# The last product by seven products of halves for the last 1280 tokens

## The chip, the core and the metric

One core of a Trainium2 chip runs the whole program. The metric is the device time of one execution in microseconds (us). Engines are named as the profile names them: PE multiplies matrices (PEld loads its stationary operand), DVE, ACT and POOL work on elements, SP issues the DMAs. All run their own instructions in the order in which the program gives them, and wait for each other by semaphores.

## The reference

Three blocks follow each other: an attention over 32 memory slots, a gated layer of width 1536, and a second layer of width 2048. The change is in the second layer's last product, `g @ w_out`: 2304 tokens of 2048 gated values times 2048 x 512 weights.

```python
def _moe2_ref(x, w_in, w_out) -> np.ndarray:
    h = x @ w_in
    g = h * (1.0 / (1.0 + np.exp(-1.702 * h)))
    return (g @ w_out).astype(np.float32)
```

The weights arrive as float64.

## The kernel before, in words

Every product is made of three passes over operands that are split into two parts: hi is the operand rounded to the type that PE takes, lo is the float32 rest, and the passes are hi·hi, lo·hi and hi·lo. `hi_lo` makes the parts: an ACT copy gives hi, and `combine` (DVE or POOL, whichever a planner finds sooner) subtracts it from the source. `PASSES` names the three.

The order of all instructions on all engines is made beforehand by a planner, `Order`: streams of work with priorities yield an engine and an estimated duration, and the stream that can start first is written out. Costs are those of the functions `dve`, `act` and `pool`. The engines then keep that order, whatever the real durations are.

The product with `w_in` already goes by seven products of halves for four (the function `step` with `PRODUCTS`, line 1062 of the profile: matmuls of 384 columns). `gate` applies the activation and stores the gated values to a DRAM tensor `g2d`, by SP's queue. The same queue loads the weights' float64 words into two buffers `raw`, and loads the gated values back.

The last product is `proj2` (line 1170): 18 tiles of 128 tokens, each 16 chunks of 128 of the 2048 values, three passes, 512 columns: 864 matmuls. `load_gated` loads 384 tokens by half of the 16 chunks (1.5 MB) into `acc`; `split_gated` makes hi and lo of 128 tokens and 8 chunks at a time (elements 128x1024, PE's stationary operand; SBUF names attn, wab_hl, vhl and whl_a, whichever old buffer lends the room). The weights' chunks are decoded from float64 words by `decode_piece`, one chunk of 128 x 512 at a time: an ACT Abs, a max (DVE or POOL, line 392), three DVE instructions on bits (lines 396, 400 and 405), then hi by ACT (line 282) and lo (line 276). Ten chunks go to the buffer y, three to g, two to whl_b, the last to eff_b.

The first six tiles are the front: PE takes them by quarters of the chunks, chunk 0 to 3 for all six tiles, then 4 to 7, and so on, since the weights' chunks are still being decoded. The other twelve follow tile by tile. `proj2_out` copies a finished bank out by ACT (line 268), and four DMAs store it.

Of the kernel before, what the change touches and what calls it, by code (L numbers as in the profile page):

```python
# [8 lines left out]
F32 = mybir.dt.float32  # L9
F32R = mybir.dt.float32r  # L10
U32 = mybir.dt.uint32
AF = mybir.ActivationFunctionType
# [139 lines left out]
def tile_mem_attention_moe_moe2(  # L152
# [38 lines left out]
    NG2 = F2 // (G2 * P)  # L191
    N2 = 384
    NP = NT // (2 * N2)
    KH = F2 // P // 2

    N1 = 512
    HT = NT // 2
# [11 lines left out]
        return Slots([pl.tile(shape, dt, name=f"{name}{i}") for i in range(n)])  # L209

    g2d = dram.tile([F2, NT], F32, name="g2d")

    banks = [psum.tile([P, 512], F32, name=f"bank{i}") for i in range(8)]
    bank_m, bank_a = Slots(banks[:3]), Slots(banks[3:])
# [163 lines left out]
    def decode_piece(t, i, name, part, n, m):  # L378

        plain = name[:2] == ("wab", 0)  # L380
        if plain:
            wt[name] = yield "slot", wab0_s
            t = max(t, wt[name][1])
        raw = loaded.pop(("raw", i))
        lw, hw = (raw[0][:, :, j].rearrange("p (n f) -> p n f", n=n) for j in range(2))
        mf = m[0].rearrange("p (n f) -> p n f", n=n)
        mu = mf.bitcast(U32)

        t, _ = yield ACT, t, act(512)
# [13 lines left out]
        t, _ = yield DVE, t, dve(512)  # L403
        dst = wt[name][0].rearrange("p (n f) -> p n f", n=n) if plain else mf
        nc.vector.scalar_tensor_tensor(
            out=dst.bitcast(U32), in0=lw, scalar=29, in1=mu, op0=ALU.logical_shift_right, op1=ALU.bitwise_or
        )
        raw_of(i).release(raw, t)
        if plain:
            dm_s.release(m, t)  # L410
            od.mark(t, *name, part)
        elif name[0] == "in":
            decoded[name, part] = m
            od.mark(t, "decoded", name, part)
            if part == 1:
                od.spawn(PW if name[1] else PW0, combine_weights(name[1]))
        elif name[0] == "o2":
            c = name[1]
            t = max(t, (yield "mark", "room", *name))
            t = yield from hi_lo(t, wo2[c][:, HI], wo2[c][:, LO], m[0], DM)  # L420
            dm_s.release(m, t)
            od.mark(t, "wo2", c)
        else:
            if part == 0:
                wt[name] = yield "slot", slots_of[name[0]]
                od.mark(wt[name][1], "place", name)
            t = max(t, (yield "mark", "place", name))
            yield from split_weights(t, name, part, wt[name][0], m, dst, n)
# [267 lines left out]
    def give(slots_, views):  # L696
        slots_.free += [[x, now()] for x in views]
# [199 lines left out]
        "P5": (S1, T1), "P6": (S2, T2), "P7": (S3, T3),  # L897
    }
    yc, win, wo2 = {}, {}, []
    win_s, hb_s, f_s, sb_s = Slots(), Slots(), Slots(), Slots()  # L900
# [5 lines left out]
    CN, FN, SN = 2 * DM, KH * N2, 2 * KH * P  # L906

    def parted(flat):

# [5 lines left out]

    def spare():
        return next(x for x in (whl_a, big["whl_b"]) if x is not wt["o1", NG1 - 1][0])

    def place(p, operands):
        for b in operands:  # L920
# [19 lines left out]
    def room_kept():  # L940

        n = KD * 2 * N2
        for r in range(2):
            yield "mark", "yc", 0, r
        give(hb_s, views(acc, N2, 6))
        give(dm_s, views(acc, DM, 1, 6 * N2))
        for r in range(2):
            yield "mark", "yc", 1, r
        give(hb_s, views(acc, N2, n // N2, n))
        for r in range(2):  # L950
            yield "mark", "yc", 2, r
        give(f_s, views(acc, FN, 1, 2 * n))

    def room_gated():

# [2 lines left out]
    def room_projected():  # L958

        nonlocal p2  # L960
        p2.release()
        p2 = tc.alloc_tile_pool(name="p3", bufs=1, reuse_waits="tile")
        rest = p2.tile([P, 6 * YN], F32R, name="rest")
        for i, x in enumerate(views(rest, YN, 6), 19):
            yc[2][i // 4][i // 2 % 2][i % 2] = x
        place(2, range(7))
# [4 lines left out]
            wo2.append(x.rearrange("p (i f) -> p i f", i=2))  # L971

    def room_split(*flat):
        give(sb_s, [x.rearrange("p (i c t) -> p i c t", i=2, c=KH) for x in flat])

    def room_last():

        used = wt["o1", NG1 - 1][0]
        room_chunks(*views(g1_m, CN, 3), *views(used, CN, 2), *views(big["eff_b"], CN, 1))
        room_split(*views(big["wab"], SN, 2), big["vhl"], spare())  # L980
# [138 lines left out]

    units = list(range(0, NT, N2))

    FRONT = 2
    parts = [(i, h) for h in range(2) for i in range(FRONT)]
    parts += [(i, h) for i in range(FRONT, len(units)) for h in range(2)]

    def load_gated():
        n = KH // G2
        for i, h in parts:  # L1130
            for g in range(h * n, (h + 1) * n):
                for j in range(2):
                    t = yield "mark", "g2", (g, i // 2), j, i % 2
            s = yield "slot", f_s
            f = s[0].rearrange("p (c t) -> p c t", c=KH)
            o = units[i]
            nc.sync.dma_start(
                out=f, in_=g2d[h * KH * P:(h + 1) * KH * P, o:o + N2].rearrange("(c p) t -> p c t", p=P)
            )
            od.load(max(t + 2500.0, s[1]), KH * P * N2 * 4, "f", i, h)  # L1140
            loaded["f", i, h] = s, f

    def split_gated():
        for i, h in parts:
            t = yield "mark", "f", i, h
            slot, f = loaded.pop(("f", i, h))
            for s in range(N2 // P):
                b = yield "slot", sb_s
                t2 = yield from hi_lo(max(t, b[1]), b[0][:, HI], b[0][:, LO], f[:, :, s * P:(s + 1) * P], KH * P)
                loaded["sb", i, h, s] = b  # L1150
                od.mark(t2, "sb", i, h, s)
            f_s.release(slot, t2)

    def proj2(tiles, cuts):

        ps = {}
        for o, e in cuts:
            h = o // KH
            for i, s in tiles:
                t = yield "mark", "sb", i, h, s  # L1160
                for c in range(o, e):
                    t = max(t, (yield "mark", "wo2", c))
                b = loaded["sb", i, h, s]
                if o == 0:
                    t, ps[i, s] = yield PE, t, 680 * (e - o), bank_m
                else:
                    t, _ = yield PE, t, 680 * (e - o)
                for c in range(o, e):
                    for n, (mv, sw) in enumerate(PASSES):
                        nc.tensor.matmul(  # L1170
                            ps[i, s][0], b[0][:, sw, c - h * KH, :], wo2[c][:, mv],
                            start=(c == n == 0), stop=(c == 2 * KH - 1 and n == 2),
                        )
                if e % KH == 0:
                    sb_s.release(b, t)
                if e == 2 * KH:
                    od.spawn(0, proj2_out(t, units[i] // P + s, ps[i, s]))

    def proj2_out(t, it, ps):
        m = yield "slot", dm_s  # L1180
# [26 lines left out]
    def main():  # L1207
# [79 lines left out]
        for q in order[1:]:  # L1287
            yield from quad(*q)
            if q == (NG2 - 1, 0):
                room_chunks(*views(big["y0"], CN, 10))  # L1290
            if q == (NG2 - 1, 1):
                room_split(*views(attn_m[0], SN, 2), *views(attn_m[1], SN, 2))
# [71 lines left out]
```

## Time and profile before

| what | us |
|---|---|
| median of 3 runs (lowest, highest) | 806.04 (805.52, 806.71) |
| profiled execution, its own time | 806.18 |
| its span, from the first to the last instruction | 804.40 |
| PE, busy | 782.6 |
| DVE, ACT, POOL, busy | 552.6, 386.6, 318.8 |
| last product on PE (line 1170) | 198.3 |

The span is what the trace shows; the profiled execution's own time is 1.78 us longer. Busy times add up per engine over stages of very different kinds, so the stage is what has to be read.

### The profile page before, as it was taken

How to read it: one execution, taken by the hardware profiler on the slowest of the kernel's cores; microseconds unless marked ns; L12 is line 12 of the kernel's file. 1: busy time of each engine (PE TensorE's matmuls, PEld its weight loads, DVE VectorE, ACT ScalarE, POOL GpSimd, SP SyncE). 2: the span in 40 equal slices, each digit the busy share in tenths (PEclk: the TensorE clock that was granted, in tenths of full speed). 3: DMA queues.
4: the chain of work that ended last, by engine and by line, in shares of the span. 5: the costliest groups of instructions: out<-in, count | busy, mean ns of one | idle time of the engine just before them, and what ended most of it. 6: DMA issues, size and time to landing. Idle time of an engine off the chain costs nothing. (4 is left out here: it accounts for less than half of the span.)

```text
span 804.4 us, 13239 instructions
## 1 busy us (share of the span) xinstructions
PE 782.6 (97%) x4928; PEld 703.0 (87%) x4928; DVE 552.6 (69%) x983; ACT 386.6 (48%) x839; POOL 318.8 (40%) x309
## 2 busy tenths in 40 slices
PE   8989999999999999999989999999999999999997
PEld 7777788899989899989978999999998878888886
DVE  4888978989988976964999877766795853212100
ACT  4567767554655545543765554554554542222200
POOL 1224235655634435432899474444376420000000
PEclk9999999999999999999999999999999999999999
DMA  8866401233230210220011326754559556323001
GB/s 292 305 205 195 147 1 53 80 105 109 76 105 28 80 52 27 67 66 1 1 45 49 136 79 214 249 170 161 170 167 342 168 198 211 115 81 118 23 17 39
DMA packets 59327, 95.48 MB, mean 119 GB/s; under 512 B 5248, under 2 KB 42112, under 8 KB 59264
## 3 DMA queue, kind: packets, MB, share of 16 engines
q1 hardware_dynamic: 58432, 93.84, 35.5%
q10 hardware_dynamic: 832, 0.82, 0.3%
q8 instruction: 38, 0.62, 0.3%
q14 instruction: 25, 0.20, 0.1%
HBM read 71.04 MB, written 23.59 MB: 118 GB/s over the span
## 5 line engine op out<-in xcount | busy, mean ns | idle before, releaser
L1104 DVE TENSOR_TENSOR acc<-bank,acc 128x384 f32<-128x384 f32 x168 | 86.9, 549 | 32.8 <-PE bank L1062 18.3
L1114 ACT ACTIVATE acc<-acc 128x384 f32<-128x384 f32 x96 | 48.1, 520 | 55.2 <-DVE acc L1104 54.9
L1170 PE MATMUL bank<-y,attn 128*128 128x512 f32 x300 | 70.8, 391 | 0.0
L1170 PEld LDWEIGHTS bank<-y,attn 128*128 128x128 f32 x300 | 56.3, 188 | 12.3
L276 POOL TENSOR_TENSOR y<-gr,y 128x288 fp32r<-128x288 f32 x43 | 37.7, 879 | 63.9 <-ACT y L282 63.7
L815 DVE TENSOR_TENSOR gr<-bank,gr 128x288 f32<-128x288 f32 x96 | 43.0, 449 | 25.6 <-PE bank L799 18.1
L832 PE MATMUL bank<-g,whl_b 128*128 128x288 f32 x384 | 55.6, 302 | 4.3 <-POOL g L276 2.0
L832 PEld LDWEIGHTS bank<-g,whl_b 128*128 128x128 f32 x384 | 53.3, 193 | 6.0 <-POOL g L276 2.8
L799 PE MATMUL bank<-attn,eff 128*128 128x288 f32 x384 | 55.2, 297 | 1.0 <-ACT eff L770 0.7
L276 DVE TENSOR_TENSOR attn<-acc,attn 128x1024 fp32r<-128x1024 f32 (+1 forms) x24 | 28.8, 1202 | 39.6 <-ACT attn L282 39.6
L799 PEld LDWEIGHTS bank<-attn,eff 128*128 128x128 f32 x384 | 52.2, 188 | 3.1 <-ACT eff L770 0.9
L812 ACT ACTIVATE gr<-bank 128x288 f32<-128x288 f32 x96 | 38.1, 399 | 32.3 <-PE bank L799 32.0
L276 POOL TENSOR_TENSOR g<-gr,g 128x288 fp32r<-128x288 f32 x37 | 35.6, 967 | 44.4 <-ACT g L282 44.1
L855 PE MATMUL bank<-y,whl_a 128*128 128x512 f32 (+1 forms) x240 | 51.5, 370 | 0.0
L855 PEld LDWEIGHTS bank<-y,whl_a 128*128 128x128 f32 x240 | 41.9, 188 | 8.0
L276 POOL TENSOR_TENSOR wab_hl<-dm,wab_hl 128x256 fp32r<-128x256 f32 (+1 forms) x31 | 29.3, 955 | 38.7 <-ACT wab_hl L282 36.4
L282 ACT ACTIVATE y<-gr 128x288 fp32r<-128x288 f32 x48 | 21.3, 444 | 43.5 <-DVE gr L815 43.3
L799 PE MATMUL bank<-attn,eff_b 128*128 128x288 f32 x288 | 40.8, 296 | 1.3 <-DVE acc L886 1.1
L875 DVE TENSOR_TENSOR acc<-bank,acc 128x512 f32<-128x512 f32 (+1 forms) x72 | 37.9, 548 | 5.1 <-PE bank L855 4.5
L799 PEld LDWEIGHTS bank<-attn,eff_b 128*128 128x128 f32 x288 | 39.0, 188 | 2.4 <-DVE acc L886 1.6
L390 ACT ACTIVATE dm<-raw 128x512 f32<-128x512 f32 x41 | 26.9, 667 | 23.5 <-DMA raw<-in_moe_w_b_dram 11.7
L392 POOL TENSOR_SCALAR dm<-dm 128x512 f32<-128x512 f32 x17 | 27.3, 1610 | 26.9 <-ACT dm L390 26.0
(287 smaller groups left out, 1941.1 us busy)
## 6 DMA issues: line engine op xcount, KB each, us to landing
g2d<-acc SPq DMA_DIRECT2D x96, 192.0 KB, 2.4
acc<-g2d SPq DMA_DIRECT2D x12, 1536.0 KB, 7.0
raw<-in_moe_w_out_dram SPq DMA_DIRECT2D x28, 512.0 KB, 4.0
raw<-in_moe_w_in_dram SPq DMA_DIRECT2D x16, 512.0 KB, 3.9
raw<-in_moe_w_a_dram SPq DMA_DIRECT2D x20, 256.0 KB, 2.8
raw<-in_moe_w_b_dram SPq DMA_DIRECT2D x20, 256.0 KB, 3.1
q<-in_q_dram SPq DMA_DIRECT2D x8, 576.0 KB, 6.4
out_dram<-dm SPq DMA_DIRECT2D x56, 64.0 KB, 1.7
```

The lines of the kernel that those rows point to most:

```text
L276: (nc.gpsimd if e == POOL else nc.vector).tensor_tensor(out=dst, in0=in0, in1=in1, op=op)
L390: nc.scalar.activation(out=mf, in_=hw.bitcast(F32), func=AF.Abs)
L392: (nc.vector if e == DVE else nc.gpsimd).tensor_scalar(out=mf, in0=mf, scalar1=2.0 ** -15, scalar2=None, op0=ALU.max)
L799: nc.tensor.matmul(ps[0][:, :U], e[c][:, sw, i * CW + j * P:i * CW + (j + 1) * P], attn(b, mv, c, u * U, U), start=(n == 0), stop=(n == 3 ...
L812: nc.scalar.activation(out=gr[0], in_=pa_[0][:, :U], func=AF.Copy)
L815: nc.vector.tensor_tensor(out=gr[0], in0=pb[0][:, :U], in1=gr[0], op=ALU.mult)
L832: nc.tensor.matmul(ps[0][:, :U], w[:, sw, j, mb * P:(mb + 1) * P], g1[0][:, j, mv, :], start=(n == 0), stop=(n == 3 * G1 - 1),)
L855: nc.tensor.matmul(ps[0][:, :e - o], w[:, sw, j, mb * P:(mb + 1) * P], g1_all[mv][:, j, o:e], start=(n == 0), stop=(n == 3 * G1 - 1),)
L875: nc.vector.tensor_tensor(out=dst, in0=ps[0][:, a - o:z - o], in1=dst, op=ALU.add)
L1104: nc.vector.tensor_tensor(out=s[0], in0=ps[0][:, :N2], in1=x[0], op=ALU.add)
L1114: nc.scalar.activation(out=c[0], in_=c[0], func=AF.Gelu_apprx_sigmoid)
L1170: nc.tensor.matmul(ps[i, s][0], b[0][:, sw, c - h * KH, :], wo2[c][:, mv], start=(c == n == 0), stop=(c == 2 * KH - 1 and n == 2),)
```

## The change

The first three units of 256 tokens (six tiles, the front) and a fourth unit are still multiplied tile by tile. The last five units (1280 tokens) are each taken as a 2 x 2 block product: two tiles of tokens, and even and odd chunks of each pair of chunks, against the halves of the 512 columns. `proj2_seven` makes seven products in place of eight, 24 matmuls of 256 columns each (two halves h of four chunk pairs, three passes), 840 matmuls for the five units. `sums_gated` makes the tokens' four sums (`MERGE`) and splits all seven operands. `sums_out` adds the products up: one ACT copy and seven DVE additions a unit.

The weights' sums T1 to T4 need float32 values of the weights. Each decoded chunk is now also written by SP's queue to a DRAM tensor `w2d` (256 KB), and `load_pair` reads two chunks at a time back (512 KB), makes four sums of 128x256 and splits each into hi and lo; both go into rooms that the older stage leaves (`blocks`). The chunk's buffer (dm) is kept until its write is done.

The operand buffers hold 4 chunks in place of 8 (`K4`): splits of 128x512, six slots of them. Loads of gated values are 256 tokens by 4 chunks (512 KB) in the front, and by 8 chunks (1 MB) after. From `room_last` on, the planner no longer puts DVE at a disadvantage against POOL (`W2`).

```diff
+W2 = 0.0
+PT = 28
...
-            t = yield from hi_lo(t, wo2[c][:, HI], wo2[c][:, LO], m[0], DM)
-            dm_s.release(m, t)
-            od.mark(t, "wo2", c)
+            nc.sync.dma_start(out=w2d[c * P:(c + 1) * P, :], in_=m[0])
+            od.mark(t + 2500.0, "w2d", c)
+            t2 = yield from hi_lo(t, wo2[c][:, HI], wo2[c][:, LO], m[0], DM)
+            dm_s.release(m, max(t + 2500.0, t2))
+            od.mark(t2, "wo2", c)
...
     def room_last():
 
+        od.handicap[DVE] = W2
...
-        give(f_s, views(acc, FN, 1, FN))
+        n = KD * 2 * N2
+        give(f_s, views(acc, FN, 1, n + 2 * FN))
+        give(fw_s, views(acc, 2 * FN, 1, n))
+        give(tb_s, views(acc, 2 * DM, 2))
+        for p in range(F2 // P // 2):
+            od.spawn(PT, load_pair(p))
+        yield "mark", "front"
+        give(fw_s, views(acc, 2 * FN, 2, n + 2 * FN))
...
+    MERGE = {
+        S1: (A22, A21, A22, ALU.add, (A22,)), S3: (A21, A11, A21, ALU.subtract, ()),
+        S2: (A11, A22, A11, ALU.subtract, (A11,)), S4: (A12, A12, A11, ALU.subtract, (A12,)),
+    }
+    HOME = {A11: A11, A12: A12, A22: A22, S1: A22, S3: A21, S2: A11, S4: A12}
+    LAST = ("P4", "P1", "P2", "P5", "P7", "P6", "P3")
...
+        for name in LAST:
+            a = PRODUCTS[name][0]
+            for h in (0, 2 * K4):
+                t, f = ts[h], parts[h][1]
+                if a in MERGE:
+                    dst, in0, in1, op, before = MERGE[a]
+                    for x in before:
+                        t = max(t, (yield "mark", "sw", i, h, x))
+                    ts[h] = t = yield from combine(t, f[dst], f[in0], f[in1], op, n)
+                yield from split_part(t, f[HOME[a]], "sw", i, h, a)
...
+    def load_pair(p):
+
+        t = max((yield "mark", "w2d", 2 * p), (yield "mark", "w2d", 2 * p + 1))
...
+        nc.sync.dma_start(
+            out=x.rearrange("p k j f -> p k (j f)"),
+            in_=w2d[2 * p * P:(2 * p + 2) * P, :].rearrange("(k p) f -> p k f", p=P),
+        )
...
+        for i, (dst, in0, in1) in enumerate(
+            ((b11, b12, b11), (b12, b22, b12), (b22, b22, b11), (b21, b21, b22))
+        ):
+            t = yield from combine(t, dst, in0, in1, ALU.subtract, n)
+            od.spawn(PT, split_t(t, wo2_t[p][i], dst, p, i))
...
+        for name in LAST:
+            a, b = PRODUCTS[name]
+            for h in (0, 2 * K4):
+                t = yield "mark", "sw", i, h, a
...
+                for c in range(K4):
+                    for n, (mv, sw) in enumerate(PASSES):
+                        nc.tensor.matmul(
+                            ps[name][0][:, :NB], x[0][:, sw, c, :], moving(b, h // 2 + c, mv),
+                            start=(h == c == n == 0), stop=(h > 0 and c == K4 - 1 and n == 2),
+                        )
...
-        tiles = [(i, s) for i in range(len(units)) for s in range(N2 // P)]
-        n = FRONT * N2 // P
-        yield from proj2(tiles[:n], [(o, o + KH // 2) for o in range(0, 2 * KH, KH // 2)])
-        for o in range(n, len(tiles), N2 // P):
-            yield from proj2(tiles[o:o + N2 // P], [(0, KH), (KH, 2 * KH)])
+        yield from proj2([(i, s) for i in range(NF) for s in range(2)])
+        for i in range(NF, NW):
+            yield from (proj2([(i, 0), (i, 1)]) if i < NS else proj2_seven(i))
```

How the change moves instructions, in three places. First PE, where the first unit by seven products begins. Before, the tiles behind the front go on with 512 columns:

```order
L1170 MATMUL bank_77<-y_1430,wab_hl 128x512 x24
L1170 MATMUL bank_76<-y_1430,wab_hl 128x512 x24
L1170 MATMUL bank_74<-y_1430,vhl 128x512 x24
L1170 MATMUL bank_77<-y_1430,whl_a 128x512 x6
L1170 MATMUL bank_77<-g_94,whl_a 128x512 x9
```

Now, behind the fourth unit's last chunks (y, g, whl_b and eff_b hold the weights' chunks; the other names hold their sums):

```order
L1287 MATMUL bank_77<-g_95,attn_92 128x512 x3
L1287 MATMUL bank_77<-whl_b,attn_92 128x512 x6
L1287 MATMUL bank_77<-eff_b,attn_92 128x512 x3
L1318 MATMUL bank_75<-wab_hl,attn_92 128x256 x6
L1318 MATMUL bank_75<-vhl,attn_92 128x256 x3
L1318 MATMUL bank_75<-whl_a,attn_92 128x256 x3
```

From there to the end every matmul has 256 columns.

Second DVE, at the decoding of the last chunk, the one that goes to eff_b. Before (dm and acc are the buffers of the chunk in decoding; vhl, wab_hl and attn are gated values being split):

```order
L405 SCALAR_TENSOR_TENSOR dm_84<-raw_78,dm_84 128x512
L276 TENSOR_TENSOR wab_hl<-acc,wab_hl 128x1024
L396 TENSOR_SCALAR acc<-acc 128x512
L400 SCALAR_TENSOR_TENSOR acc<-raw_79,acc 128x512
L405 SCALAR_TENSOR_TENSOR acc<-raw_79,acc 128x512
L276 TENSOR_TENSOR vhl<-acc,vhl 128x1024
```

Now (the rows of 128x256 are the weights' sums and their splits):

```order
L280 TENSOR_TENSOR whl_b<-acc,whl_b 128x512
L396 TENSOR_SCALAR dm_85<-dm_85 128x512
L400 TENSOR_SCALAR dm_85<-dm_85 128x512
L280 TENSOR_TENSOR acc<-acc 128x256
L404 SCALAR_TENSOR_TENSOR dm_85<-raw_79,dm_85 128x512
L280 TENSOR_TENSOR attn_92<-acc,attn_92 128x512
L280 TENSOR_TENSOR acc<-acc 128x256
L280 TENSOR_TENSOR eff_b<-acc,eff_b 128x256
L280 TENSOR_TENSOR acc<-acc 128x256
L280 TENSOR_TENSOR eff_b<-acc,eff_b 128x256
L409 SCALAR_TENSOR_TENSOR dm_85<-raw_79,dm_85 128x512
L280 TENSOR_TENSOR eff_b<-dm_85,eff_b 128x512
```

Sums of the weights stand between the steps of the last chunk's decoding, its max (line 396 there) is DVE's and no longer POOL's, and its lo is DVE's too.

Third SP's queue, at the raw loads of chunks 10 and 11. Before:

```order
L1116 DMA g2d<-acc 128x384 x4
L1137 DMA acc<-g2d 128x8x384 x2
L308 DMA raw_78<-in_moe_w_out_dram 128x1024
L308 DMA raw_79<-in_moe_w_out_dram 128x1024
L308 DMA raw_78<-in_moe_w_out_dram 128x1024
```

Now:

```order
L1141 DMA g2d<-acc 128x384 x3
L1156 DMA acc<-g2d 128x4x256
L1250 DMA acc<-w2d 128x2x512 x2
L312 DMA raw_80<-in_moe_w_out_dram 128x1024
L424 DMA w2d<-dm_84 128x512
L312 DMA raw_79<-in_moe_w_out_dram 128x1024
L424 DMA w2d<-dm_83 128x512
```

Two loads of 1.5 MB ahead of the raw loads have become one of 0.5 MB and two reads of `w2d`, and the writes of `w2d` stand between.

## Rows read from the trace of the kernel before

**Rows 1.** The page: busy time of each engine and its share of the span.

```profile
PE 782.6 (97%) x4928; PEld 703.0 (87%) x4928; DVE 552.6 (69%) x983; ACT 386.6 (48%) x839; POOL 318.8 (40%) x309
```

**Rows 2.** The chain that ended last, in order of time: start, length, what.

```profile
601.53 198.33 PE bank L1170 x864
```

**Rows 3.** Window: PE, PEld, DVE, ACT, POOL busy; clock, DMA share, GB/s.

```profile
600.00:650.00 50.00, 50.00 (x222) 41.24 (x221) 36.51 (x46) 23.09 (x32) 27.45 (x16) 1.00 0.75 262
```

**Rows 4.** Timeline around 652 us: start, length; the last weight chunk meets PE.

```profile
651.24 0.63 ACT L282 ACTIVATE eff_b<-acc 128x512 fp32r<-128x512 f32 x1 [3.38 <-DVE acc L405]
...
651.95 1.29 POOL L276 TENSOR_TENSOR eff_b<-acc,eff_b 128x512 fp32r<-128x512 f32 x1 [2.48 <-ACT eff_b L282]
...
652.94 1.08 PE L1170 MATMUL bank<-eff_b,vhl 128*128 128x512 f32 x3
```

**Rows 5.** Timeline of PE, the only three stretches of 256-column matmuls.

```profile
256.56 2.99 PE L855 MATMUL bank<-y,whl_a 128*128 128x256 f32 x24
...
312.15 2.92 PE L855 MATMUL bank<-y,whl_b 128*128 128x256 f32 x23
...
366.76 2.87 PE L855 MATMUL bank<-y,whl_a 128*128 128x256 f32 x23
```

**Rows 6.** Timeline of DVE, four instructions that follow each other.

```profile
633.62 0.43 DVE L396 TENSOR_SCALAR dm<-dm 128x512 uint32<-128x512 uint32 x1
634.08 0.69 DVE L400 SCALAR_TENSOR_TENSOR dm<-raw,dm 128x512 uint32<-128x512 uint32 x1
634.68 1.22 DVE L276 TENSOR_TENSOR attn<-acc,attn 128x1024 fp32r<-128x1024 f32 x1
635.82 1.10 DVE L405 SCALAR_TENSOR_TENSOR dm<-raw,dm 128x512 uint32<-128x512 uint32 x1
```

**Rows 7.** DVE's groups from 405 to 440 us, with POOL busy throughout: busy, mean ns.

```profile
L276 DVE TENSOR_TENSOR attn<-acc,attn 128x384 fp32r<-128x384 f32 x7 | 7.4, 1060 | 0.0
L1104 DVE TENSOR_TENSOR acc<-bank,acc 128x384 f32<-128x384 f32 x9 | 4.7, 544 | 0.0
```

**Rows 8.** DVE's groups from 601 to 655 us that hold most of its delay.

```profile
L400 DVE SCALAR_TENSOR_TENSOR dm<-raw,dm 128x512 uint32<-128x512 uint32 x6 | 5.2, 872 | 0.1
...
L405 DVE SCALAR_TENSOR_TENSOR dm<-raw,dm 128x512 uint32<-128x512 uint32 x6 | 5.0, 826 | 0.1
...
L396 DVE TENSOR_SCALAR acc<-acc 128x512 uint32<-128x512 uint32 x2 | 3.0, 1510 | 1.4 <-POOL acc L392 1.4
...
L405 DVE SCALAR_TENSOR_TENSOR acc<-raw,acc 128x512 uint32<-128x512 uint32 x3 | 2.7, 901 | 0.1
L392 DVE TENSOR_SCALAR dm<-dm 128x512 f32<-128x512 f32 x3 | 2.6, 882 | 4.5 <-ACT dm L390 4.4
```

**Rows 9.** Windows in which PE waited, and the one behind it.

```profile
420.00:425.00 5.00, 1.72 (x9) 1.02 (x8) 4.97 (x7) 1.71 (x4) 4.73 (x6) 0.97 0.44 138
425.00:430.00 5.00, 4.89 (x25) 4.65 (x25) 5.00 (x9) 3.24 (x8) 4.89 (x5) 0.68 0.36 103
```

**Rows 10.** Timelines of DVE and ACT where the last product has begun.

```profile
604.49 1.47 DVE L1104 TENSOR_TENSOR acc<-bank,acc 128x384 f32<-128x384 f32 x3
...
608.18 0.65 ACT L390 ACTIVATE dm<-raw 128x512 f32<-128x512 f32 x1
...
623.62 0.66 ACT L390 ACTIVATE dm<-raw 128x512 f32<-128x512 f32 x1 [3.45 <-DMA raw<-in_moe_w_out_dram]
```

**Rows 11.** The page's DMA issues, gated values loaded: count, size, us to landing.

```profile
acc<-g2d SPq DMA_DIRECT2D x12, 1536.0 KB, 7.0
```

**Rows 12.** Groups by form over the whole span: busy, mean ns of one.

```profile
L276 POOL TENSOR_TENSOR acc<-acc 128x256 f32<-128x256 f32 x3 | 2.2, 748 | 0.0
...
L392 POOL TENSOR_SCALAR dm<-dm 128x512 f32<-128x512 f32 x17 | 27.3, 1610 | 26.9 <-ACT dm L390 26.0 <-DVE acc L1104 0.9
...
L875 DVE TENSOR_TENSOR acc<-bank,acc 128x256 f32<-128x256 f32 x36 | 13.9, 413 | 1.3 <-PE bank L855 1.0
...
L855 PE MATMUL bank<-y,whl_a 128*128 128x256 f32 x48 | 6.0, 279 | 0.0
```

More of the change, by code (lines that the diff above doesn't have):

```diff
@@ L984, in room_last @@
                     yield "mark", "g2", q, j, u
-        give(f_s, views(acc, FN, 1, FN))
+        n = KD * 2 * N2
[6 more added lines that the diff above has]
+        give(fw_s, views(acc, 2 * FN, 2, n + 2 * FN))
+        for p in range(F2 // P // 2):
+            yield "mark", "wt", p
+        give(dm_s, views(acc, DM, 4))
     def split(t, dst, src, n, *key):
@@ L1143, in split_gated, with gated_part @@
-    def split_gated():
-        for i, h in parts:
+    NF, NS, NW = 3, 4, NT // NB
+    def gated_part(s, i, o, e):
+        t = 0.0
+        for g in range(o // G2, (e - 1) // G2 + 1):
+            for n in range(i * NB // N2, ((i + 1) * NB - 1) // N2 + 1):
+                for j in range(2):
+                    t = max(t, (yield "mark", "g2", (g, n // 2), j, n % 2))
+        f = s[0].rearrange("p (c t) -> p c t", c=e - o)
+        nc.sync.dma_start(
+            out=f, in_=g2d[o * P:e * P, i * NB:(i + 1) * NB].rearrange("(c p) t -> p c t", p=P)
+        )
+        od.load(max(t + 2500.0, s[1]), (e - o) * P * NB * 4, "f", i, o)
+        loaded["f", i, o] = s, f
@@ new lines, in load_gated, with split_part @@
+    def load_gated():
+        for o in range(0, 4 * K4, K4):
+            for i in range(NF):
+                s = yield "slot", f_s
+                yield from gated_part(s, i, o, o + K4)
+        for i in range(NF, NW):
+            for o in (0, 2 * K4):
+                s = yield "slot", fw_s
+                yield from gated_part(s, i, o, o + 2 * K4)
+    def split_part(t, src, *key):
+        b = yield "slot", sb_s
+        loaded[key] = b
+        od.spawn(4, split_into(max(t, b[1]), b, src, key))
@@ new lines, in split_into @@
+    def split_into(t, b, src, key):
+        t = yield from hi_lo(t, b[0][:, HI], b[0][:, LO], src, K4 * P)
+        od.mark(t, *key)
+    def split_gated():
+        for o in range(0, 4 * K4, K4):
+            for i in range(NF):
+                t = yield "mark", "f", i, o
+                slot, f = loaded.pop(("f", i, o))
+                for s in range(2):
+                    yield from split_part(t, f[:, :, s * P:(s + 1) * P], "sb", i, o, s)
+                for s in range(2):
+                    t = max(t, (yield "mark", "sb", i, o, s))
+                f_s.release(slot, t)
+        od.mark(t, "front")
+        for i in range(NF, NW):
+            yield from (split_whole(i) if i < NS else sums_gated(i))
@@ L1145, in split_gated, with split_whole @@
+    def split_whole(i):
+        for h in (0, 2 * K4):
             t = yield "mark", "f", i, h
             slot, f = loaded.pop(("f", i, h))
[L1147 to L1154, printed above, removed]
+            for o in range(0, 2 * K4, K4):
+                for s in range(2):
+                    yield from split_part(t, f[:, o:o + K4, s * P:(s + 1) * P], "sb", i, h + o, s)
+            for o in range(0, 2 * K4, K4):
+                for s in range(2):
+                    t = max(t, (yield "mark", "sb", i, h + o, s))
+            fw_s.release(slot, t)
@@ L1174, in proj2 @@
[L1174 to L1177, printed above, removed]
+                            ps[i, s][0], b[0][:, sw, c - o, :], wo2[c][:, mv],
+                            start=(c == n == 0), stop=(c == 4 * K4 - 1 and n == 2),
+                        )
+                sb_s.release(b, t)
+                if o == 3 * K4:
+                    od.spawn(0, proj2_out(t, 2 * i + s, ps[i, s]))
@@ new lines, in sums_out @@
+    def sums_out(i, ps):
+        x = yield "slot", dm_s
+        o0 = yield "slot", dm_s
+        o1 = yield "slot", dm_s
+        lo, hi = slice(0, NB), slice(NB, 2 * NB)
+        t = yield "mark", "done", i, "P1"
+        t, _ = yield ACT, max(t, x[1]), act(NB, True)
+        nc.scalar.activation(out=x[0][:, lo], in_=ps["P1"][0][:, :NB], func=AF.Copy)
+        bank_m.release(ps["P1"], t)
+        base = max(t, o0[1], o1[1])
+        for name, dst, src, last in (
+            ("P2", o0[0][:, lo], x[0][:, lo], True), ("P6", x[0][:, hi], x[0][:, lo], True),
+            ("P7", x[0][:, lo], x[0][:, hi], True), ("P5", o0[0][:, hi], x[0][:, hi], False),
+            ("P5", o1[0][:, hi], x[0][:, lo], True), ("P4", o1[0][:, lo], x[0][:, lo], True),
+            ("P3", o0[0][:, hi], o0[0][:, hi], True),
+        ):
+            t = yield "mark", "done", i, name
+            base, _ = yield DVE, max(t, base), dve(NB)
+            nc.vector.tensor_tensor(out=dst, in0=ps[name][0][:, :NB], in1=src, op=ALU.add)
+            if last:
+                bank_m.release(ps[name], base)
+            if name == "P4":
+                dm_s.release(x, base)
+                store(2 * i + 1, o1[0])
+                dm_s.release(o1, base + 2500.0)
+        store(2 * i, o0[0])
+        dm_s.release(o0, base + 2500.0)
```

115 lines of the change are left out of this document (81 added, 34 removed).

## The prediction

> **What bounds the kernel now.** I read the page first: PE is busy for 97% of the span, and no other engine for more than 69% [rows 1]. The chain that ended last then says which work sets the end: from 601.53 us on it is PE alone, 864 matmuls of the last product in 198.33 us, 229.5 ns each [rows 2]. The window of 600 to 650 us shows PE without a pause, at the full clock (2.4 GHz), while DVE is busy for 36.5 us of 50, POOL for 27.5 and the DMA engines for 75% [rows 3]. So the last product costs what PE's instructions cost, as long as its operands are there in time.
>
> Whether they are is seen on the timeline around 652 us. PE comes to the last weight chunk (eff_b) at 652.94, and the chunk's lo, POOL's 1.29 us, ends at 653.24 [rows 4]. The front's last quarter has no slack: whatever makes chunk 15 later makes PE wait.
>
> **PE's own work.** The five units were 10 tiles of 48 matmuls: 480 x 229.5 ns = 110.2 us. They become 5 x 168 = 840 matmuls of 256 columns. The trace has 72 of that size, each with a new stationary operand, in three stretches. The first lasts 2.99 us for 24, and a single one 279 ns from start to end [rows 5, 12]: (2.99 - 0.28) / 23 = 118 ns from one to the next. The others give 120 and 118 ns. With 118.5 ns the five units cost 99.5 us (98.9 to 100.8). PE gains 10.6 us (9.4 to 11.3).
>
> The stationary loads are hidden in those stretches; I take it that they stay hidden.
>
> **What the front has to do more.** DVE, POOL, ACT and the queue now also make the weights' sums while chunks 8 to 15 are decoded. PE reaches chunk 15 at 652.9 as before, since the front's order of tiles and quarters on PE is the same. So I add up what DVE has to do before chunk 15's lo, which is now its own instruction. From the place where the additions of the older product end, DVE's order has 23 instructions of 128x512 with two inputs in SBUF, 37 of 128x256 of that kind, 16 of the two-input bit instructions and 13 of the one-input ones. From one start to the next the one-input form takes 0.46 us, the two-input bit form 0.60, and a 128x1024 subtraction 1.14 [rows 6]; I take 0.61 for 128x512 and, by 413 ns less the 0.07 by which neighbours overlap, 0.34 for 128x256 [rows 12]. That is 14.0 + 12.6 + 9.6 + 6.0 = 42.2 us.
>
> It can begin when the older additions are done (605.96) and chunk 8 has passed ACT, which before was from 608.18 to 608.83, behind a long split that is now two short ones [rows 10]. I take 607.6. Alone, DVE would finish chunk 15 at 649.8, 3.1 us early.
>
> It is not alone. POOL has in the same stretch 16 instructions of 128x256 (748 ns [rows 12]), three of 128x512 (1.29 us [rows 4]) and three of the max (1.6 us [rows 12]): 12.0 + 3.9 + 4.8 = 20.7 us. What POOL's work does to DVE is seen from 405 to 440 us, where both are busy throughout: a DVE instruction of 128x384 with its inputs in SBUF takes 1060 ns, one that reads PSUM 544 [rows 7]. So DVE advances at 0.51 of its pace while POOL is busy, and loses 0.49 x 20.7 = 10.1 us at the most. The least I take from the front as it is. There the five groups hold an excess over 0.43 us (one input) and 0.69 us (two) of 1.1 + 0.8 + 2.2 + 0.6 + 1.4 = 6.1 us, against 27.45 us of POOL [rows 8, 3]: 0.22 us for each, 4.6 us here. DVE is nearer to always busy than it was there, and not as full as at 405 us: I take the middle, 7.3 us. DVE will also wait for ACT and for loads: 1.5 us (0 to 3). Before, it had more of such waits in this stretch, 4.5 us for ACT's first step of a chunk alone [rows 8], and ACT waited for a raw load until 623.62 [rows 10]; with DVE behind, most of that is gone.
>
> Chunk 15 is then ready at 649.8 + 7.3 + 1.5 = 658.6, and PE waits for 5.7 us (1.5 to 10.0). Behind it on PE stands everything else, and nothing shortens it later: the wait goes into the end.
>
> The Trainium skill, "SBUF — State Buffer" (Who interferes with whom), says of this pair of engines that it is not a sharing at all: a DVE instruction with two SBUF inputs and a GpSimd instruction that reads SBUF exclude each other for the whole instruction. By that rule DVE's 42.2 us and POOL's 20.7 us would simply add. The trace disagrees in part: at 405 us DVE still advances at half pace beside a POOL that never stops [rows 7].
>
> **The clock.** After windows in which PE was busy for only 1.72 us of 5, the granted clock fell to a mean of 0.68 in the next [rows 9]. Between the two levels of 2.4 and 1.2 GHz that is 3.2 us at the lower, and 0.3 us more in the window of 0.97: 3.5 us at half speed, 1.7 us lost. A wait of 5.7 us in one piece should do the same. For a wait under 3 us I take nothing.
>
> **The DMAs.** 16 writes of 256 KB and 8 reads of 512 KB are 8 MB more. At 262 GB/s for a share of 0.75 [rows 3] that is 23 us of all DMA engines, spread over the front and the 25 us ahead of it; the 3 MB that stood ahead of the raw loads of chunks 10 and 11 are cut to 0.5 MB and two reads of 0.5. Each read of `w2d` waits in SP's queue for its two writes and for the sums of the pair two before, and the raw loads wait behind it. By DVE's order these sums stand early enough each time, so I count nothing beyond the 1.5 us. `w2d` writes also keep the chunk's buffer; with four of these and two raw buffers, the raw buffers bind first.
>
> **The five units.** PE needs 168 x 118.5 ns = 19.9 us for one. DVE has 14 splits and 7 additions, 14 x 0.61 + 7 x 0.34 = 10.9 us; POOL has all 8 sums of a unit, 8 x 1.3 = 10.4 us, and if all of that delays DVE as at 405 us, DVE needs 16.0. Both stay below 19.9, so PE hides them. The loop that could be longer is that of the buffers: a half of gated values (1 MB) lands, at most 7.0 us by the 1.5 MB loads [rows 11], its first operand is split (1.3), six sums follow on POOL (7.8, or 9.6 if delayed), and the last split (1.3) gives the buffer back: 17.4 to 19.4 us. Close, but hidden. The end keeps its form: a DVE addition of 0.41 us [rows 12] in place of an ACT copy, then four stores. I count 0.
>
> **Sum.** The profiled execution took 806.18 us (span 804.40 and 1.78 around it), 0.14 above the median of the runs shown. 806.2 - 10.6 + 5.7 + 1.7 = 803.0 us. With the wait between 1.5 (and no clock loss) and 10.0, and PE's gain between its bounds, the forecast reaches from 796.4 to 808.5.
>
> **The rivals.**
> - *Chunk 15 is in time.* What held it before was in part the queue: a raw load that stood behind 3 MB of gated values landed only at 623.6 [rows 10]. If the shorter loads bring the chunks that much earlier, DVE never gets behind, and only the 10.6 us count: 795.6. Against it: DVE's 42.2 us must lie between 607.6 and 652.9 with no more than 3.1 us of delay, less than the least I found.
> - *DVE and POOL exclude each other* (slower). In the front as it is, two one-input instructions took 1510 ns where one alone takes 430 [rows 8, 6]: they waited for nearly all of a POOL instruction. If all did, chunk 15 would come at 607.6 + 42.2 + 20.7 = 670.5, PE would wait for 17.6 us, and the time would be 806.2 - 10.6 + 17.6 + 1.7 = 814.9. It decides from a wait of 8.9 us on, where wait and clock eat the gain. The Trainium skill's "SBUF — State Buffer" (Who interferes with whom) states this as the rule; the trace bears it out by half [rows 7].
> - *The buffers' loop binds the five units.* If a load and the sums made 22 us of it, each unit behind the first would wait for about 2 us: 8 us more than the forecast, 811.
> - *The change doesn't save on PE*: the stationary loads take 41.24 us for 221, 187 ns each [rows 3]; if 256 columns did not cover them, the five units would cost 840 x 187 ns = 157 us, and the time would be 806.2 - 110.2 + 157 + 7.4 = 860. The three stretches speak against it plainly [rows 5].
>
> **How the numbers follow.** The forecast (chunk 15 late by 1.5 to 10 us) has 0.47, chunk 15 in time 0.23, the exclusion or as long a wait from another cause (over 9 us) 0.19, the buffers' loop 0.08, no saving 0.03. A measurement here can tell 0.2% (1.6 us) from no change: faster is below 804.4, slower above 807.6. Of the forecast's 0.47 some 0.31 lie below, 0.13 within, 0.03 above; chunk 15 in time is faster; of the others 0.27 are slower and 0.03 within. Faster 0.54, same 0.16, slower 0.30. The range that leaves out 2 in 10 is 796 to 812; the likeliest case's own is 796.4 to 808.5.
>
> **What would show it.** Matmuls of 256 columns 118 to 120 ns apart; one wait of PE of about 6 us at chunk 15, before the first matmuls on eff_b, released by DVE; a granted clock below 1 behind it; DVE busy for 45 us or more of 600 to 650; and no waits of PE in the five units. The prediction is wrong if PE waits elsewhere in the front (for pairs or raw loads), or if DVE keeps up beside POOL.

## The result and the profile after

The change took 817.57 us (median of 4 runs, 816.31 to 818.75), beside 805.81 for the kernel before on the same chip: a ratio of 1.014 (1.0128 to 1.0152). It is slower by 11.8 us, where the forecast had it faster by 3.2 us (803.0 against the 806.2 of the profiled execution), and it lies above the range. The profiled execution has a span of 816.2 us.

The page's busy line of the changed kernel, beside [rows 1]:

```profile
PE 780.3 (96%) x5288; PEld 716.7 (88%) x5288; DVE 638.0 (78%) x1138; ACT 419.2 (51%) x932; POOL 382.7 (47%) x359
```

PE is busy for 2.3 us less, in a span that is 11.8 us longer; DVE and POOL have 85 and 64 us more to do.

The chain that ended last in the changed kernel, from the last product on (start, length, what); L1287 is the tile-by-tile part, L1318 the seven products. The lines left out between the first and the last ones are shown further on.

```profile
600.75 19.24 PE bank L1287 x84
...
671.39 38.94 PE bank L1287 x158
710.33 91.71 PE bank L1318 x770
...
803.74 7.18 PE bank L1318 x58
810.94 0.42 DVE acc L1346
```

Before, PE alone made this chain in 198.33 us [rows 2]. Now it takes 210.2 (600.75 to 810.94), and for 51 us of it (619.99 to 671.39) it runs through other engines: in that stretch PE is no longer what everything waits for.

The windows of the changed kernel, with the same columns as [rows 3]:

```profile
600.00:650.00 50.00, 45.47 (x187) 35.41 (x185) 41.83 (x74) 23.00 (x49) 20.14 (x18) 0.97 0.76 247
650.00:700.00 50.00, 39.89 (x159) 31.42 (x160) 28.59 (x48) 20.34 (x40) 8.43 (x8) 0.90 0.62 194
700.00:750.00 50.00, 50.00 (x380) 48.09 (x379) 29.80 (x40) 20.78 (x35) 24.30 (x17) 1.00 0.39 117
```

PE is idle for 4.5 us of the first stretch and 10.1 of the second, at a lowered mean clock in both, and never in the third, where the seven products have begun. What it waited for from 600 to 700 us (total, times, longest):

```profile
PE bank L1287 <- ACT eff_b L286: 8.1, 1, 8.1
...
PE bank L1287 <- DVE attn L280: 5.0, 4, 1.5
```

With two shorter kinds (1.0 for splits by ACT, 0.3 for chunk 15's lo) that is 14.4 us: 8.4 at chunk 15, as [rows 4] let expect, and 6.0 ahead of it, for splits of the tokens' values that came late from the same engines. PE's timeline at chunk 15 and in a stretch of seven products:

```profile
670.32 0.79 PE L1287 MATMUL bank<-eff_b,attn 128*128 128x512 f32 x1 [8.11 <-ACT eff_b L286]
671.39 1.22 PE L1287 MATMUL bank<-eff_b,attn 128*128 128x512 f32 x2 [0.28 <-DVE eff_b L280]
...
712.67 2.29 PE L1318 MATMUL bank<-y,attn 128*128 128x256 f32 x18
714.79 0.89 PE L1318 MATMUL bank<-g,attn 128*128 128x256 f32 x6
...
715.87 1.93 PE L1318 MATMUL bank<-y,attn 128*128 128x256 f32 x15
717.64 0.53 PE L1318 MATMUL bank<-g,attn 128*128 128x256 f32 x3
```

The last four rows say 712.67 to 714.79 for 18 matmuls and 715.87 to 717.64 for 15, from one row's start to the next: 118 ns for one, as the stretches of [rows 5] gave. All 840 take from 710.33 to 810.92 by the chain, 119.8 ns each. PE's saving is there. What went wrong lies ahead of 671 us, in the chain's middle. The pieces that matter (of a sum, `acc` L280, only the start is in the chain):

```profile
638.64 0.60 DVE dm L409
...
639.65 4.40 DMA w2d<-dm
...
644.59 3.79 DMA acc<-w2d
...
648.40 0.04 DVE acc L280
...
648.75 0.42 DVE dm L400
...
654.64 0.68 DVE dm L409
...
655.74 5.22 DMA w2d<-dm
...
661.09 3.86 DMA acc<-w2d
...
664.97 0.04 DVE acc L280
...
665.32 0.68 DVE dm L404
...
669.00 0.60 DVE dm L409
```

This is a loop: DVE ends a chunk's decode (L409), the chunk is written to DRAM (4.4 and 5.2 us), the pair is read back (3.8 and 3.9 us), the pair's sum runs on DVE, and only then the next steps of a chunk's decode, which stand behind the sum in DVE's fixed order. It goes round twice, from 638.64 to 669.60. The waits of DVE from 600 to 700 us (8.3 of the 11.6 us lie ahead of 671) say the same, and those of SP's queue from 600 to 680, which holds the read for the write:

```profile
DVE acc L280 <- DMA acc<-w2d: 11.6, 4, 3.3
```

```profile
SPq L1250 <- DMA w2d<-dm: 10.4, 3, 4.8
```

### The profile page after: what moved, and what is told of

The parts are those of the page before. It is cut to its first block, busy times and chain, and to the rows that moved or that the text cites. A ratio compares the mean times of both kernels' runs of the same rounds, so it can differ in the third digit from the quotient of the medians.

```text
span 816.2 us, 14487 instructions
## 1 busy us (share of the span) xinstructions
PE 780.3 (96%) x5288; PEld 716.7 (88%) x5288; DVE 638.0 (78%) x1138; ACT 419.2 (51%) x932; POOL 382.7 (47%) x359
## 5 line engine op out<-in xcount | busy, mean ns | idle before, releaser
L280 POOL TENSOR_TENSOR acc<-acc 128x512 f32<-128x512 f32 (+2 forms) x70 | 96.7, 1403 | 95.8 <-DVE attn L280 42.9
L280 DVE TENSOR_TENSOR attn<-acc,attn 128x512 fp32r<-128x512 f32 (+2 forms) x105 | 101.7, 988 | 41.3 <-ACT attn L286 41.2
L286 ACT ACTIVATE attn<-acc 128x512 fp32r<-128x512 f32 (+2 forms) x119 | 70.0, 606 | 68.4 <-PE bank L1318 25.8
L280 POOL TENSOR_TENSOR y<-gr,y 128x288 fp32r<-128x288 f32 x43 | 37.9, 883 | 63.6 <-ACT y L286 63.4
L1287 PE MATMUL bank<-y,attn 128*128 128x512 f32 x240 | 59.2, 399 | 6.3 <-DVE attn L280 5.0
L1287 PEld LDWEIGHTS bank<-y,attn 128*128 128x128 f32 x240 | 45.0, 190 | 18.7 <-DVE attn L280 7.8
L280 POOL TENSOR_TENSOR g<-gr,g 128x288 fp32r<-128x288 f32 x37 | 35.6, 968 | 44.4 <-ACT g L286 44.3
L280 POOL TENSOR_TENSOR wab_hl<-dm,wab_hl 128x256 fp32r<-128x256 f32 (+1 forms) x31 | 29.6, 967 | 40.4 <-ACT wab_hl L286 36.5
```

The costliest lines, as they stand in the source:

```text
L280: (nc.gpsimd if e == POOL else nc.vector).tensor_tensor(out=dst, in0=in0, in1=in1, op=op)
L286: nc.scalar.activation(out=hi, in_=src, func=AF.Copy)
L1287: nc.tensor.matmul(ps[i, s][0], b[0][:, sw, c - o, :], wo2[c][:, mv], start=(c == n == 0), stop=(c == 4 * K4 - 1 and n == 2),)
```

## The experiments

Two theories at first. **A**: the trip through DRAM (write, then read) stands in DVE's order ahead of the decodes and splits that PE needs. **B**: DVE's and POOL's extra work slow each other. Each kernel was compared with the kernel before on its own chip (medians 806.25 to 806.92 us); ratios are to that. Where a time is said to be less than that of the change, medians are subtracted; by the ratios these differences are the same within 0.5 us. The experiments stand in the order of the argument: 5, 10 and 11 were run last. In the quoted expectations VectorE is DVE, GpSimd is POOL and TensorE is PE.

**1. e1_no_round_trip.**

```diff
+    qf = q.rearrange("b (h x) s d -> (b h) (x s d)", x=1).rearrange("a (r c) -> (a r) c", c=DM)
...
-            in_=w2d[2 * p * P:(2 * p + 2) * P, :].rearrange("(k p) f -> p k f", p=P),
+            in_=qf[2 * p * P:(2 * p + 2) * P, :].rearrange("(k p) f -> p k f", p=P),
```

> The changed kernel, with the eight reads of pairs taken from the input q (float32, same size and rows) in place of w2d: the writes of w2d stay, every engine's order stays, and only the wait of a read for its two writes goes. The weights' sums are made of other numbers, so the output is not the reference's. Theory A (the front is late because each decoded chunk has to be written to DRAM and read back, 4 to 5 us and 3.8 us, before DVE's next instruction in its order can go on): DVE's waits for pair reads (8.3 us) go, chunk 15 comes 11 to 14 us earlier, at 657 to 660, and the time is 803 to 806. Theory B (DVE and POOL hold each other up): little changes, 814 to 818.

813.2 us, 1.008 (1.0065 to 1.0095): 4.4 us less than the change, and in neither theory's range. DVE still waited 4.8 us for the reads themselves (11.6 in the change, from 600 to 700 us). Waiting for the write is part of the cause and not all of it.

**2. e2_brief_pool.**

```diff
+    def combine_brief(t, dst, in0, in1, op, n):
...
+        if e == POOL:
+            dst, in0, in1 = dst[:, :8], in0[:, :8], in1[:, :8]
...
-            t = yield from combine(t, dst, in0, in1, ALU.subtract, n)
+            t = yield from combine_brief(t, dst, in0, in1, ALU.subtract, n)
...
```

> The changed kernel, with POOL's instructions of the weights' sums and their lo parts cut from 256 columns to 8: order and waits stay, POOL's work in the front nearly goes. The rest of those columns is left as it was, so the output is not the reference's. Theory B: DVE's delay of some 10 us beside POOL goes, 806 to 809. Theory A: DVE still waits for every pair read, and gains only what POOL takes inside the loop of decoding, write, read and sum: 813 to 817.

813.06 us, 1.0079 (1.0062 to 1.0096): 4.5 us less, where B alone had 806 to 809 and A 813 to 817. What POOL did to DVE is seen in one group of DVE, the 20 sums of 128x256 (from 607 us until about chunk 15, at 671 us in the change and 664 here: busy, mean ns, idle before), first of the change and then of this kernel:

```profile
L280 DVE TENSOR_TENSOR acc<-acc 128x256 f32<-128x256 f32 x20 | 11.3, 569 | 8.3 <-DMA acc<-w2d 8.3
```

```profile
L1247 DVE TENSOR_TENSOR acc<-acc 128x256 f32<-128x256 f32 x20 | 8.4, 418 | 10.1 <-DMA acc<-w2d 9.9
```

The sums are faster, and DVE loses part of that by waiting longer for the reads.

**3. e3_sums_late.**

```diff
-        t = max((yield "mark", "w2d", 2 * p), (yield "mark", "w2d", 2 * p + 1))
+        t = max((yield "mark", "w2d", 2 * p), (yield "mark", "wo2", F2 // P - 1))
```

> The changed kernel, with the pairs' reads and sums held back until chunk 15 is decoded; the planner makes a new order. Both theories: the front waits 0 to 2 us as before the change, PE's gain of 9.7 us stays, 796 to 799. If the 64 instructions of the sums don't fit between chunk 15 (653) and the first unit by seven products (689), PE waits there instead, by up to 10 us: 800 to 808.

810.24 us, 1.0039 (1.0024 to 1.0054). The 796 to 799 of both theories was wrong. All of the front up to chunk 15 ran without a wait of PE, though the writes of `w2d` stayed there, but now PE waited behind it, 7.2 us in 9 pieces. DVE's timeline where it reaches the first sum:

```profile
652.14 0.88 DVE L280 TENSOR_TENSOR acc<-acc 128x256 f32<-128x256 f32 x2 [5.09 <-DMA acc<-w2d]
```

What PE waited for:

```profile
PE bank L1287 <- DVE attn L280: 5.9, 6, 2.2
PE bank L1287 <- ACT attn L286: 1.3, 3, 1.0
```

The first pair's read landed 5.1 us after DVE had reached its sum, and the splits of the tokens' values (`attn`) stood behind that sum. The wait had moved, not gone.

**4. e5_both** (the edits of 1 and 2 together).

> Both cuts together: the pair reads take rows of q in place of the float32 copy (so the sums have wrong values and their reads wait for no write), and GpSimd's instructions of the sums touch 8 columns in place of 256 (left out: most of GpSimd's part). Alone, they took 817.6 down to 813.2 and to 813.06. Theory AB (the wait for the DRAM trip and the shared work of VectorE and GpSimd each delay the splits, one after the other): the two gains add, 817.6 - 4.4 - 4.5 = about 808.7, TensorE waits some 4 us in the front. Theory C (each cut only frees VectorE up to the same next limit, the number of instructions in its fixed order): the second cut adds little, 811 to 813. Theory D (without both, the chunks come in time, so TensorE doesn't wait until the ninth 256 tokens): 800 to 804.

807.61 us, 1.0016 (1.0006 to 1.0026): 10.0 us less than the change, where 4.4 and 4.5 were to be had singly. A and B both hold and add. PE still waited 5.4 us at chunk 15, and the chain ahead of it still runs through the pairs' reads, now of q:

```profile
647.64 7.26 DMA acc<-in_q_dram
```

With the sums ahead of chunk 15, it is late even so.

**5. e12_true_landing.**

```diff
-            od.mark(t + 2500.0, "w2d", c)
+            od.mark(t + 5500.0, "w2d", c)
...
+        od.marks["pair", p] += 500.0
```

The chunk's buffer is released by the same 5.5 us.

> The change with all its work, and two of the planner's figures set by the change's own trace: a write of the float32 copy is taken to land 5.5 us after its chunk's decode (2.5 before; the trace: 4.4 to 5.2 us and the way to the queue) and a pair's read 0.5 us later than before. The planner sets the order of the instructions by them, so the sums of a pair stand further back in VectorE's order. Theory A (the figures of the DRAM trip alone put the splits behind sums that wait): VectorE's 11.6 us of waits for pair reads mostly go, chunk 15 is some 4 us or more earlier, time 811 to 813, about what the reads without a write to wait for gave (813.2). Theory AB (the rest is the sums' work beside GpSimd ahead of chunk 15): no better than 809. Theory E (later sums only meet the splits of the tokens further back): 814 to 817.

812.42 us, 1.0073 (1.0056 to 1.009). DVE's waits for pair reads between 600 and 700 us fell from 11.6 to 3.6 us, with all the work in place. So the order, made by landing times that were too short, was the cause of these waits. That gives 5 us and no more, as A had it: the sums were still ahead of chunk 15, and PE still waited 9.2 us from 600 to 700 us.

**6. e6_small_buffers**: all units tile by tile, with the change's smaller buffers and loads and no sums.

```diff
-            nc.sync.dma_start(out=w2d[c * P:(c + 1) * P, :], in_=m[0])
...
-            od.spawn(PT, load_pair(p))
...
-    NF, NS, NW = 3, 4, NT // NB
+    NF, NS, NW = 3, NT // NB, NT // NB
```

> The changed kernel with all nine units multiplied tile by tile: no w2d, no pairs, no seven products; what is left of the change is the smaller operand buffers, the smaller loads and the planner's new handicap. If these are harmless in the front, as both theories have it: 804.5 to 807.5. If the smaller splits and loads themselves delay chunk 15: 809 or more.

808.76 us, 1.0026 (1.0017 to 1.0036), between the two ranges, without a wait of PE in the last product. Its row in the chain:

```profile
602.20 200.16 PE bank L1281 x864
```

The 864 matmuls of 512 columns of [rows 2] now stand 231.7 ns apart in place of 229.5. The smaller loads don't delay PE; that is 1.8 us, all that this kernel is slower by. The pace differs from one pair of operands to the next: 15 matmuls of `y` with `attn` stood 233.3 ns apart here (from 699.71 to 703.21), 30 of `y` with `wab_hl` before 227.0 (from 711.66 to 718.47). Whether the buffers' places make it was not tried.

**7. e8_no_sums.**

```diff
-            nc.sync.dma_start(out=w2d[c * P:(c + 1) * P, :], in_=m[0])
...
-        nc.sync.dma_start(
-            out=x.rearrange("p k j f -> p k (j f)"),
...
-        for i, (dst, in0, in1) in enumerate(
-            ((b11, b12, b11), (b12, b22, b12), (b22, b22, b11), (b21, b21, b22))
-        ):
...
```

> The float32 copy's writes, the pair reads, the sums of the weights and their splits are left out; the seven products read what lies in the blocks of the sums (so the last 1280 tokens are wrong), and TensorE, the sums of the tokens and all stores stay as in the change. Theory A, B and AB alike: every wait in the front goes, and the time is that of before less the 10.6 us of TensorE, plus the slower pace of the smaller buffers that the sixth kernel showed (1.9 us on 864 matmuls, some 0.9 on the 384 and about 1.1 on the 840) and 0.8 more after the last matmul: 806.9 - 10.6 + 2.0 + 0.8 = about 799. The rival that the seven products themselves or the tokens' sums cost something that the front's waits hide: 803 or more.

797.48 us, 0.989 (0.9875 to 0.9905), 1.5 us below the 799 that was expected. The last product has no wait of PE and lasts until 790.7 us. So the weights' sums, with their writes, reads and splits, cost the change 20.1 us, and all that is left of it (seven products, sums of tokens, small buffers, another end) gains 8.8.

**8. e7_late_landing** (3, and a pair's read planned to land later).

```diff
         od.load(max(t, m[1]), 2 * P * DM * 4, "pair", p)
+        od.marks["pair", p] += LAND
```

with `LAND = 4000.0` ns.

> As the third kernel (sums only after chunk 15's split is issued, 810.2 us), and the planner takes a pair's read to land 4.0 us later than it did, since the trace showed 4.3 to 7.3 us in place of 3.4: more splits of tokens stand ahead of the first sums in VectorE's order; nothing is left out. Theory A (the splits are late because they stand behind sums that wait for a read): VectorE's 11.7 us of waits for reads mostly go, TensorE's waits between 653 and 692 us fall from 7.2 us to under 3, time 804 to 806. Theory B (the sums' work itself, slowed beside GpSimd, is too much for these 40 us): still 5 to 8 us of TensorE waits, 808 to 811.

806.42 us, 1.0002 (0.9993 to 1.0012): no difference from before. PE's waits for splits between 653 and 692 us are gone, as A expected, but DVE's waits for reads are not: 9.1 us of 11.7 are left. More splits stand ahead of the sums, so that these waits no longer reach PE. A new wait of PE came in their place, at the first seven products: 4.1 us for the last sums (`y`), with a lowered clock behind it (a mean of 0.93 from 700 to 710 us). PE's waits from 640 to 700 us:

```profile
PE bank L1319 <- ACT y L286: 2.1, 1, 2.1
PE bank L1319 <- DVE y L280: 2.0, 1, 2.0
```

**9. e9_four_units** (8, and four units by seven products).

```diff
-    NF, NS, NW = 3, 4, NT // NB
+    NF, NS, NW = 3, 5, NT // NB
```

> As e7, and only the last four units of 256 tokens (1024 tokens) by seven products; the fifth is computed tile by tile, which adds 96 matmuls of 512 columns and takes away 168 of 256, 22.0 - 19.9 = 2.1 us of TensorE's gain, and gives the sums 22 us more. Theory A: the order of VectorE's instructions between 650 and 690 us is almost that of e7, so its waits stay and the time is e7's plus 2.1. Theory B (too much work before the seven products start): waits of the splits stay too, since they stand in the same order, but any wait of TensorE for the last sums before the first seven products is gone; time e7's less 0 to 3.

798.88 us, 0.991 (0.9895 to 0.9924): faster than both kernels, with no part left out. Neither theory's number held (808.5 by A, 803.4 to 806.4 by B), though B named the wait that went, that for the last sums. From the last product on, the chain is PE's alone:

```profile
600.63 110.90 PE bank L1288 x480
711.53 80.06 PE bank L1319 x672
...
791.61 0.42 DVE acc L1347
```

DVE's timeline in this kernel:

```profile
650.31 1.34 DVE L280 TENSOR_TENSOR acc<-acc 128x256 f32<-128x256 f32 x3 [4.43 <-DMA acc<-w2d]
...
686.64 1.35 DVE L280 TENSOR_TENSOR acc<-acc 128x256 f32<-128x256 f32 x3 [4.57 <-DMA acc<-w2d]
...
694.21 0.43 DVE L280 TENSOR_TENSOR y<-acc,y 128x256 fp32r<-128x256 f32 x1 [0.15 <-ACT y L286]
```

DVE still waits 4.4 and 4.6 us for reads, in all 10.7 us. But enough splits stand ahead of each sum, and the last block of the sums (`y`) is ready by 694.6, while the first seven products begin at 711.5. Such waits now cost nothing: the time is that of e8, which has no sums at all, plus 1.4 us, and the unit that is given up accounts for 2.1.

**10. e11_late_four_units** (9 without the later landing).

> Sums after chunk 15 (as the third kernel, 810.2 us) and four units by seven products, with the planner's own landing times: the fast version without the 4.0 us later landing. Theory A (in the order by the planner's times, splits of tokens stand behind sums that wait for reads, 7.2 us of TensorE's waits between 653 and 692 us): these waits stay, 806 to 811. Theory F (only the last sums before the first seven products cost time, and the later units free them): 798 to 800.

810.87 us, 1.0058 (1.0043 to 1.0073). PE waited 6.0 us for splits, as in experiment 3. Four units alone don't help.

**11. e10_four_units_early** (the change, four units).

> The change with one number altered: four units of 256 tokens by seven products in place of five, the sums of the weights as early as in the change. The arithmetic gives back 2.1 us (96 matmuls of 512 columns at 229.5 ns for 168 of 256 at 118.5). Theory AB (the sums stand ahead of the last chunks, and the front's waits make the loss): the front is unchanged, so 817.6 + 2.1 = 818 to 820. Theory F (what made the fast version fast was the time between the front and the first seven products): 800 to 810.

818.85 us, 1.0159 (1.0139 to 1.0179), as AB had it, and 7.9 us of wait at chunk 15: the loss stays where it was.

## Why the prediction was wrong

**PE's gain was right in the main.** 118.5 ns (118 to 120) from one 256-column matmul to the next was forecast, and 118 on `y` and 119.8 in the mean were seen. Without the weights' sums the whole change gains 8.8 us (e8) where 10.6 were counted; most of the difference is pace: in e8 the 384 matmuls of 512 columns stood 230.7 ns apart in place of 229.5, and the 840 of 256 columns 119.8 in the mean in place of 118.5, together 1.5 us.

**The step that failed** is the one on the DMAs: "By DVE's order these sums stand early enough each time, so I count nothing beyond the 1.5 us." So the term of 1.5 us (0 to 3) for DVE's waits was far too small: 11.2 us were measured. The sums do stand early in DVE's order, but that is what hurts: the two on the chain came behind a write and a read that together took 8.2 and 9.1 us, and the next decode, the next chunk and so PE waited behind them. I had looked at what was queued behind the reads in SP's queue and not at what was queued behind the sums on DVE. The sum for chunk 15, with what was measured (from 607 to 671 us):

- work of DVE: 42.2 us, the forecast's own (its 89 instructions, of the same forms, are there);
- delay beside POOL: 11.0 us by the durations (15 splits of 128x512 at 894 ns in place of 690, 20 sums at 569 in place of 413, and so on), a little over the bound of 10.1, where 7.3 was taken;
- waits: 8.3 us for pair reads and 2.9 for ACT, where 1.5 was taken and 3 was the bound for both.

DVE's groups by form in that stretch, beside the one shown at experiment 2 (busy, mean ns, idle before), and the stretch as a window:

```profile
L280 DVE TENSOR_TENSOR attn<-acc,attn 128x512 fp32r<-128x512 f32 x15 | 13.4, 894 | 0.0
...
L396 DVE TENSOR_SCALAR dm<-dm 128x512 f32<-128x512 f32 x4 | 1.7, 421 | 2.9 <-ACT dm L394 2.9
```

```profile
607.00:671.00 64.00, 49.63 (x199) 37.76 (x197) 52.41 (x90) 28.99 (x62) 24.68 (x22) 0.93 0.68 225
```

That is 64.4 us in place of 51.0, and 607.0 + 64.4 = 671.4, where DVE's lo of chunk 15 did end (670.66 to 671.34). The waits are the larger part of the error, 9.7 us; the delay beside POOL adds 3.7. Experiments 1, 2 and 4 show both parts: 4.4 us, 4.5 us, and 10.0 together. What remains of the 20.1 us, some 10 (e5 against e8), is lost because the sums and their reads stood ahead of chunk 15 at all: in e9 the same work lies later and costs nothing. How these 10 us divide between the reads, which e5 still has on its chain, and the sums' own instructions was not measured.

**The wait of PE** was forecast as one of 5.7 us at chunk 15. It was 8.4 there and 6.0 ahead of it: the splits of the tokens' values were late too, since they stood behind sums as well. So the premise that PE reaches chunk 15 "at 652.9 as before" failed too: it came there at 662.2. Waits "elsewhere in the front" were one of the signs of being wrong that the prediction had named, and another of its signs failed: DVE was busy for 41.8 us of 600 to 650 and not for 45, since it waited.

**The clock** was put at 1.7 us for one wait. The granted clock fell to 1.2 GHz, half the full 2.4, twice in the front (windows with the columns of [rows 3]):

```profile
638.70:642.10 3.40, 3.40 (x8) 2.75 (x9) 3.38 (x7) 1.57 (x3) 1.04 (x1) 0.50 0.45 101
666.00:676.20 10.20, 5.60 (x12) 4.13 (x13) 6.95 (x12) 3.33 (x7) 2.55 (x3) 0.50 0.25 80
```

The first stands behind three waits of PE of 0.9, 1.0 and 1.3 us (from 632 to 639 us), where the forecast took nothing for waits under 3 us; the second begins within the wait at chunk 15. In these stretches 16 of PE's matmuls stood 427 ns apart in place of 229.5, which alone is 3.2 us.

**The five units** hid their sums, splits and loads, as forecast: no wait of PE behind chunk 15, and from 700 to 750 us PE busy for 50.00 us of 50, DVE for 29.8, POOL for 24.3. (The upper figure of the forecast's buffer loop adds up to 19.2 us and not 19.4.)

**The rivals.** The size of the loss was near that of "DVE and POOL exclude each other" (814.9), but not its mechanism: it was "as long a wait from another cause", which shared the chance of 0.19 with it. The Trainium skill, "SBUF — State Buffer" (Who interferes with whom), by whose rule such instructions of DVE and POOL exclude each other, would let all of POOL's working time there count. That is 20.7 us by the forecast's prices, and DVE's instructions were lengthened by 11.0: by the rule's whole price, an estimate, chunk 15 would be some 10 us later than by the trace. Of the others, chunk 15 was not in time, PE did not wait for the buffers' loop, and the saving on PE was there.

## What to carry to other kernels

Work that waits for a trip through DRAM must not stand in an in-order engine's stream ahead of work that the bound engine needs: look for what is queued behind the waiting instruction on every engine, not just in the DMA queue. The planner's landing times decide this: with the sums behind chunk 15, 4.0 us more in one of them was worth 3 to 4 us with five units (e3 against e7) and 12.0 with four (e11 against e9). Take them from a trace. Then give the work a deadline that it can meet: one unit fewer in the cheaper form gave up 2.1 us of PE's gain, and the time still fell by 7.5 (e7 to e9), while without the later landing it did not fall (e3 to e11).

## What the hardware showed beside that

DVE's subtractions with two inputs in SBUF grew by about the same time beside a busy POOL whether they had 256 or 512 columns, not in proportion. DVE's timeline of the changed kernel, and below it POOL's:

```profile
649.08 1.21 DVE L280 TENSOR_TENSOR attn<-acc,attn 128x512 fp32r<-128x512 f32 x1
650.22 0.95 DVE L280 TENSOR_TENSOR acc<-acc 128x256 f32<-128x256 f32 x1
...
652.24 0.41 DVE L280 TENSOR_TENSOR acc<-acc 128x256 f32<-128x256 f32 x1
...
656.03 0.69 DVE L280 TENSOR_TENSOR whl_b<-dm,whl_b 128x512 fp32r<-128x512 f32 x1
```

```profile
648.97 0.78 POOL L280 TENSOR_TENSOR acc<-acc 128x256 f32<-128x256 f32 x1 [1.10 <-DVE acc L280]
649.71 2.06 POOL L280 TENSOR_TENSOR attn<-acc,attn 128x256 fp32r<-128x256 f32 x2
```

Beside POOL, 0.41 became 0.95 and 0.69 became 1.21: 0.54 and 0.52 us more. Seven others of 256 columns from 607 to 671 us took 0.94 to 0.96 us, and six of 512 took 1.21 to 1.23. POOL had 22 instructions in that stretch, so the 11.0 us are 0.50 us for each in the mean. Taking half pace, as I did, makes short instructions look too cheap there. What sets this time is open.

The pace of matmuls changed with the operand buffers and their order, with no wait of PE: 229.5 ns before and 231.7 in e6 for 864 matmuls of one shape. Which of these makes it was not tried.
